# Weight loads cut into 64-row blocks over 128 partitions, with the bulk loads in one queue in order of need and a head built tile by tile

## The chip, the cores and the metric

The kernel runs on one core of a Trainium2 chip. The metric is the device time of one execution in microseconds (us). Each time is a median, with the lowest and highest run beside it. Profiles are of one execution. The profile calls the engines PE (TensorE, matmul), PEld (weight loads into TensorE), DVE (VectorE), ACT (ScalarE), POOL (GpSimd) and SP (SyncE). A trailing q (SPq, ACTq) names the engine's sequencer, where DMA issues appear. The kernel before ran in 207.21 us (two runs, 206.26 and 208.16).

## The reference

Layer norm of x (2048 x 448), then two branches, joined at the end. Types are bf16.

```python
def _A_ref(x, ...):                 # a diagonal state-space layer, P = 448 complex states
    dt = jnp.exp(log_dt); Lam_bar = jnp.exp(dt * Lam)
    Bu = jnp.einsum("bld,pd->blp", x, B_bar)
    for t in range(L): h = Lam_bar * h + Bu[:, t, :]
    return 2.0 * jnp.einsum("blp,dp->bld", hseq, Cmat).real + x * Dskip

def _B_ref(x, w_gate, w_up, w_down):   # a gated feed-forward, F = 1792
    h = _sigmoid(x @ w_gate) * (x @ w_up)
    return h @ w_down

xn = _layernorm(x)
out = x + _A_ref(xn, ...) * _silu(_B_ref(xn, w_gate, w_up, w_down))
```

`w_gate` and `w_up` are 448 x 1792 in DRAM, 1.6 MB each. They must be on chip before TensorE can work on the second branch.

## The kernel before

The kernel records its operations with `add(engine, cost, fn, reads, writes)`. A small scheduler (`Plan`) then orders them on each engine, by costs. So an edit of one line can also move operations that the edit doesn't name.

The contraction over 448 runs in seven steps of 64 rows. Partitions 0 to 63 hold the weights of columns 0 to 895, partitions 64 to 127 those of columns 896 to 1791. That lets two 64-row matmuls run beside each other (lines 603 and 604 of the kernel before). One "step" `m` is 7 + 7 such matmuls; it needs columns `m` of all seven row blocks.

```python
BLK = [(0, 3), (3, 7)]

def load_w(eng, k, half, b):          # one load = one 64-partition half, seven row blocks
    m0, m1 = BLK[b]
    ps = slice(half * H, half * H + H)                    # H = 64
    c0 = half * 896
    load(eng, [("w", k, half, m) for m in range(m0, m1)], ...,
         wgt[k][ps, :, m0 * P:m1 * P],
         wsrc[k][:, c0 + m0 * P:c0 + m1 * P].rearrange("(s p) f -> p s f", p=H))

load_x(0, 1); load_x(1, 1); load_x(2, 2)          # on SP
load_w("ACT", "g", 1, 0); load_w("SP", "g", 0, 0) # gate
load_w("ACT", "g", 1, 1); load_w("SP", "g", 0, 1)
load_w("ACT", "u", 1, 0); load_w("SP", "u", 0, 0) # up
load_w("SP", "u", 1, 1);  load_w("SP", "u", 0, 1)
# ... (cut)
pe_transpose(0); g_head(0, 1)                     # gate steps 0 to 2 on tile 0
pe_transpose(1); g_head(1, 2)                     # the same on tile 1
pe_transpose(2); pe_transpose(3)
columns()
for m in range(3):
    gu_mm(0, "g", m, slots0[m], 2, 4, m == 0)     # then on tiles 2 and 3 together
    gu_evac(0, "g", m, slots0[m])
tables(); coeffs()
load_x(4, 4)                                      # behind all the weights, on SP
b_load()
load("POOL", "wd", F * D * 2, wd[:], ...)         # w_down, on GpSimd's queue
load_x(8, 8, "POOL")
```

Of the kernel before, what the change touches and what calls it, by code (L numbers as in the profile page):

```python
# [18 lines left out]
D = 448  # L19
F = 1792  # L20
P = 128
# [51 lines left out]
class Plan:  # L73
# [53 lines left out]
    def solve(self, pe_from):  # L127
# [11 lines left out]
        for o in reversed(self.ops):  # L139
            for b, kind in o.suc:  # L140
                x = b.late - self._gap(o, b, kind) - o.cost
                if kind is not None and o.eng != b.eng:
                    x -= 1.5 if o.dma else 0.2
                o.late = min(o.late, x)
# [8 lines left out]
        while todo:  # L153
# [13 lines left out]
            if o.dma:  # L167
                q = dma_free[e] = max(dma_free.get(e, 0.0), o.end + 1.2) + o.dma / 200e3
                o.lat = q + 0.6 - o.end
# [13 lines left out]
def kernel(  # L183
# [73 lines left out]
    one = sb.tile([1, 1], BF16, name="one")  # L257
    pio2 = sbt("pio2", [1], FP32)
    vrow = hF_raw[0][0:1, 0:2048].rearrange("p (a b) -> p a b", a=4)
# [27 lines left out]
    def load(eng, key, nbytes, o, i, cost=0.45):  # L287
        e = {"SP": Q, "ACT": A, "POOL": G}[eng]
        add(eng, cost, lambda: e.dma_start(out=o, in_=i), w=[key] if not isinstance(key, list) else key,
            dma=nbytes, chain=True)  # L290

    def load_x(t0, n, q="SP"):
        load(q, [("x", t) for t in range(t0, t0 + n)], n * P * D * 2,
             x_all[:, t0:t0 + n, :], x_src[:, t0:t0 + n, :])

    BLK = [(0, 3), (3, 7)]

    def load_w(eng, k, half, b):
        m0, m1 = BLK[b]
        ps = slice(half * H, half * H + H)  # L300
        c0 = half * 896
        load(eng, [("w", k, half, m) for m in range(m0, m1)], H * 7 * (m1 - m0) * P * 2,
             wgt[k][ps, :, m0 * P:m1 * P],
             wsrc[k][:, c0 + m0 * P:c0 + m1 * P].rearrange("(s p) f -> p s f", p=H))
# [5 lines left out]
    add("POOL", 0.3, lambda: G.memset(warm[:], 0.0), w=["warm"])  # L310
# [3 lines left out]
    add("POOL", 0.1, lambda: G.memset(one[:], 1.0), w=["one"])  # L314
# [6 lines left out]

    add("ACT", 1.3, lambda: A.preload_act_table_set("sqrt_and_others"), w=["sqrttab"], chain=True)
    load_x(0, 1)
    load_x(1, 1)
    load_x(2, 2)
    load_w("ACT", "g", 1, 0)
    load_w("SP", "g", 0, 0)
    load_w("ACT", "g", 1, 1)
    load_w("SP", "g", 0, 1)
    load_w("ACT", "u", 1, 0)  # L330
    load_w("SP", "u", 0, 0)
    load_w("SP", "u", 1, 1)
    load_w("SP", "u", 0, 1)
    for k, vec in enumerate((A_log_dt, A_Lambda_im, A_Lambda_re, A_Dskip)):
        load("POOL", ("vrow", k), D * 2, vrow[:, k, 0:448], vec.unsqueeze(0), cost=1.0)


    def warm_mm(n):
# [3 lines left out]
        add("PE", 0.35 * n, f, r=["warm"], w=[("gu", 2)])  # L342
# [7 lines left out]
    def chain(t0, n):  # L350
# [4 lines left out]
        if t0 < TPC:  # L355
            add("DVE", 0.09, lambda: V.tensor_single_scalar(out=ve, in_=var, scalar=EPS, op=ALU.add), r=ks("mv"), w=ks("ve"))
            add("ACT", 0.2, lambda: A.activation(sd, ve, ACT.Sqrt), r=ks("ve") + ["sqrttab"], w=ks("sd"))
            add("DVE", 0.09, lambda: V.tensor_copy(out=meanf[:, t0:t0 + n, :], in_=mean), r=ks("mv"), w=ks("mf"))
# [9 lines left out]
    def norm(t):  # L368
        b = t % NXN
        if t < TPC:  # L370
# [4 lines left out]
            add("DVE", 0.085, lambda: V.tensor_copy(out=xn[b][:, 448:512], in_=xn[b][:, 0:64]),  # L375
# [18 lines left out]
    def pe_transpose(t):  # L394
# [3 lines left out]
        def f():  # L398
            for s in range(7):
                T.transpose(tp[:, s, :], xn[b][:, s * H:s * H + P], ident[:, :])  # L400
        add("PE", 0.43, f, r=[("xn", b), ("xnw", b), "ident"], w=[("acc", a)])
        add("ACT", 0.476, lambda: A.copy(out=xnT[0][:, 0:4, js], in_=tp[:, 0:4, :]),
            r=[("acc", a)], w=[("xnT", 0, t, "a")])
        add("DVE", 0.27, lambda: V.tensor_copy(out=xnT[0][:, 4:7, js], in_=tp[:, 4:7, :]),
            r=[("acc", a)], w=[("xnT", 0, t, "b")])
# [23 lines left out]
    def columns():  # L429
        a = next_acc()  # L430
        vps = flat(acc[a][:, 0:16], 4, 4)
        add("POOL", 0.3, lambda: G.tensor_copy(out=vrow[:, :, 448:512], in_=vrow[:, :, 384:448]),
            r=[("vrow", k) for k in range(4)], w=["vroww"])

        def f():
            for k in range(4):
                for i in range(4):
                    T.matmul(vps[:, k, i:i + 1], lhsT=vrow[:, k, i * P:(i + 1) * P], rhs=one[:], start=True, stop=True)
# [552 lines left out]
```

## Time and profile before

| what | kernel before |
|---|---|
| time, median (lowest to highest) | 207.21 us (206.26 to 208.16) |
| span of the profiled run, mean clock | 204.8 us, 0.979 |
| TensorE busy, VectorE busy | 186.2 us, 160.0 us |
| first gate matmul | 11.68 us |
| first gate step on all 512 columns | 22.03 us |
| first up step | 28.07 us |

The first view is the table of windows of the kernel before. Each row is a stretch in us from the start, then the stretch's length, the busy time of each engine with its count of instructions, the clock granted to TensorE as a share of full speed, the mean busy share of the core's 16 DMA engines, and GB/s moved.

```profile
core 0: us, PE busy (x) PEld busy (x) DVE busy (x) ACT busy (x) POOL busy (x), PEclk, DMA share, GB/s
0.00:5.00 5.00, 3.69 (x9) 1.34 (x10) 1.02 (x4) 1.49 (x2) 4.38 (x17) 1.00 0.57 141
5.00:10.00 5.00, 1.43 (x11) 0.59 (x9) 2.84 (x11) 0.72 (x2) 0.78 (x1) 0.84 1.12 236
10.00:15.00 5.00, 3.28 (x49) 2.92 (x50) 3.10 (x15) 0.41 (x2) 1.76 (x3) 0.50 1.08 292
15.00:20.00 5.00, 3.34 (x80) 2.96 (x81) 1.15 (x4) 2.19 (x4) 0.20 (x1) 0.98 1.03 333
20.00:25.00 5.00, 5.00 (x66) 3.44 (x64) 3.04 (x8) 4.97 (x7) 3.43 (x7) 1.00 1.10 238
25.00:30.00 5.00, 5.00 (x49) 2.58 (x46) 1.18 (x3) 3.05 (x4) 2.52 (x6) 1.00 1.40 191
```

Look at the last two columns. From 5 to 30 us all the DMA engines are taken (a share of about 1, which can go above 1 where records overlap) and 191 to 333 GB/s flow. The head is bound by data. TensorE is full only from 20 us.

The second view is the list of waits of TensorE in the kernel before (engine, line, what it waited for, us in total, times, longest).

```profile
PE gu L603 <- DMA wG<-in_B_w_gate_dram: 4.1, 1, 4.1
PE gu L603 <- ACT hF L619: 2.4, 1, 2.4
```

TensorE waits 4.1 us for the gate weights, once, and 2.4 us for a tanh on ScalarE.

The third view is part 6 of the page of the kernel before: transfers by target and source, issuing queue, count, KB each and median us from issue to landing.

```profile
wd<-in_B_w_down_dram POOLq DMA_DIRECT2D x1, 1568.0 KB, 13.6
wU<-in_B_w_up_dram SPq DMA_DIRECT2D x2, 448.0 KB, 19.4
...
x_all<-in_A_x_dram SPq DMA_DIRECT2D x1, 448.0 KB, 19.2
```

The second group of x tiles (4 to 7) stands behind the up weights on SP and lands 19.2 us after its issue. The fourth view, VectorE's timeline in the kernel before (start, duration, instruction, in brackets the idle time ahead of it and what ended it), shows VectorE in that wait:

```profile
28.82 1.15 DVE L347 BATCH_NORM_STATS2 bst<-x_all 128x6 f32<-128x448 bf16 x2 [4.07 <-DMA x_all<-in_A_x_dram]
```

### The profile page before, as it was taken

Reading aid. Unit: us, or ns where it says so; the run is one execution under the profiler, and the core shown is the slowest. Engines: PE = TensorE matmul, PEld = TensorE weight load, DVE = VectorE, ACT = ScalarE, POOL = GpSimd, SP = SyncE. Lnnn points to the kernel's source line nnn. Section 1 sums busy time; section 2 is a strip of 40 time slices with the busy share of each in tenths; the row PEclk is TensorE's granted clock in tenths of the full one; section 3 lists DMA queues with packets and bytes.
Section 4 is the critical chain, followed back from the end, with each engine's and each line's share of the span. In section 5 each row is a group of like instructions: output and inputs, shape, how many; then the busy total and the mean of one; then the engine's idle time right before and its main releaser. Section 6 shows DMA issues by size and latency. Waiting matters only on the chain.

```text
span 204.8 us, 3700 instructions
## 1 busy us (share of the span) xinstructions
PE 186.2 (91%) x1459; PEld 92.5 (45%) x1459; DVE 160.0 (78%) x304; ACT 114.6 (56%) x160; POOL 43.4 (21%) x94
## 2 busy tenths in 40 slices
PE   7267995899799999999699999999999999999992
PEld 2156652434344544444244544444445444455561
DVE  1552539999999999999999999995599799531153
ACT  2114947948999956734935943836537582510330
POOL 8130749677100017007106100000000000000000
PEclk9859999999999999999999999999999999999998
DMA  5999994345400013300311220000000000001002
GB/s 143 235 295 338 223 165 88 74 91 109 89 2 3 0 22 71 78 12 3 73 40 45 48 67 0 3 22 22 0 16 10 0 3 22 22 27 48 0 22 67
DMA packets 26946, 13.32 MB, mean 65 GB/s; under 512 B 19696, under 2 KB 26368, under 8 KB 26928
## 3 DMA queue, kind: packets, MB, share of 16 engines
q1 hardware_dynamic: 24800, 9.41, 21.6%
q0 software_dynamic: 736, 2.53, 3.9%
q10 hardware_dynamic: 1392, 1.15, 2.6%
q8 instruction: 11, 0.18, 0.4%
q14 instruction: 7, 0.06, 0.1%
HBM read 6.66 MB, written 1.84 MB: 41 GB/s over the span
## 4 chain that ended last, share of the span: by engine, by line
PE 50%; DVE 23%; DMA 13%; ACT 5%; POOL 4%; issue 2%; SPq 1%; DVEq 0%; POOLq 0%; ACTq 0%
PE gu L603 18%; DMA x_all<-in_A_x_dram 13%; PE acc L782 10%; PE acc L810 8%; PE gu L782 5%; PE gu L667 4%; DVE wv L721 4%; DVE hF L628 3%; DVE bst L347 2%; ACT sig L622 2%; DVE hF L633 2%; DVE cT L572 2%; POOL rsd L364 1%; PE acc L816 1%; POOL sdb L363 1%
## 5 line engine op out<-in xcount | busy, mean ns | idle before, releaser
L603 PE MATMUL gu<-xnT,wG 64*128 64x512 bf16 (+2 forms) x238 | 47.7, 347 | 5.0 <-DMA wG<-in_B_w_gate_dram 4.1
L603 PE MATMUL gu<-xnT,wU 64*128 64x512 bf16 x196 | 46.5, 376 | 2.4 <-ACT hF L619 2.4
L604 PE MATMUL gu<-xnT,wG 64*128 64x512 bf16 (+2 forms) x238 | 47.7, 347 | 0.0
L604 PE MATMUL gu<-xnT,wU 64*128 64x512 bf16 x196 | 46.5, 376 | 0.0
L782 PE MATMUL acc<-wd,hF 128*128 128x448 bf16 x168 | 33.8, 353 | 0.0
L603 PEld LDWEIGHTS <-wG 64*128 64x128 bf16 x238 | 21.4, 98 | 25.4 <-DMA wG<-in_B_w_gate_dram 4.2
L782 PEld LDWEIGHTS <-hF 128*128 128x128 bf16 x224 | 21.5, 98 | 21.3 <-issue 2.1
L622 ACT ACTIVATE sig<-gu 128x1024 bf16<-128x1024 f32 x21 | 21.5, 1022 | 14.5 <-PE gu L604 12.1
L603 PEld LDWEIGHTS <-wU 64*128 64x128 bf16 x196 | 17.9, 94 | 22.8 <-issue 2.1
L632 ACT CAST ub<-gu 128x1024 bf16<-128x1024 f32 x21 | 21.2, 1009 | 9.2 <-PE gu L604 9.1
L810 PE MATMUL acc<-cT,hT 128*128 128x448 bf16 x105 | 24.3, 353 | 0.0
L721 DVE TENSOR_TENSOR_SCAN wv<-c_r,st,z 128x512 bf16<-128x512 f32 x18 | 23.0, 1280 | 0.2
L604 PEld LDWEIGHTS <-wG 64*128 64x128 bf16 x238 | 21.1, 98 | 1.2 <-issue 1.0
L604 PEld LDWEIGHTS <-wU 64*128 64x128 bf16 x196 | 17.7, 94 | 3.3 <-issue 3.2
L633 DVE TENSOR_TENSOR hF<-sig,ub 128x1024 bf16<-128x1024 bf16 x21 | 14.2, 681 | 5.8 <-ACT ub L632 5.8
L347 DVE BATCH_NORM_STATS2 bst<-x_all 128x6 f32<-128x448 bf16 x16 | 9.4, 616 | 10.0 <-DMA x_all<-in_A_x_dram 10.0
L667 PE MATMUL gu<-xnT,bT 128*128 128x512 bf16 x72 | 16.9, 380 | 0.0
L792 DVE TENSOR_TENSOR g_t<-zb,sigd 128x448 bf16<-128x448 bf16 x16 | 6.1, 386 | 12.8 <-ACT zb L791 12.8
L678 ACT CAST bus<-gu 128x1024 bf16<-128x1024 f32 x12 | 12.1, 1010 | 4.8 <-PE gu L667 4.8
L810 PEld LDWEIGHTS <-hT 128*128 128x128 bf16 x119 | 10.4, 98 | 7.3 <-issue 0.4
L790 ACT ACTIVATE sigd<-acc 128x448 bf16<-128x448 f32 x12 | 6.5, 540 | 12.2 <-PE acc L782 12.2
L378 ACT ACTIVATE xn<-x_all,nmr,rsd 128x448 bf16<-128x448 bf16 x12 | 8.8, 754 | 5.6 <-POOL nmr L366 5.6
(140 smaller groups left out, 278.9 us busy)
## 6 DMA issues: line engine op xcount, KB each, us to landing
out_dram<-o_t SPq DMA_DIRECT2D x15, 112.0 KB, 1.7
wd<-in_B_w_down_dram POOLq DMA_DIRECT2D x1, 1568.0 KB, 13.6
wU<-in_B_w_up_dram SPq DMA_DIRECT2D x2, 448.0 KB, 19.4
x_all<-in_A_x_dram POOLq DMA_DIRECT2D x1, 896.0 KB, 11.4
wG<-in_B_w_gate_dram ACTq DMA_DIRECT2D x1, 448.0 KB, 6.9
wG<-in_B_w_gate_dram SPq DMA_DIRECT2D x1, 448.0 KB, 14.9
x_all<-in_A_x_dram SPq DMA_DIRECT2D x1, 448.0 KB, 19.2
xnT<-xn SPq DMA_TRANSPOSE x24, 2.4
```

The costliest lines, as they stand in the source:

```text
L347: add("DVE", 0.53, lambda: V.bn_stats(out=bst[b][:], in_=x_all[:, t, :]), r=[("x", t)], w=[("bst", b)])
L378: add("ACT", 0.65, lambda: A.activation(xn[b][:, 0:448], x_all[:, t, :], ACT.Identity, bias=nmr[:, t, :], scale=rsd[:, t, :]), r=[("x", t) ...
L603: T.matmul(gu[a][:, 0, ts], lhsT=w_[0:H, s, ms], rhs=x[0:H, s, ts], start=(s == 0), stop=(s == 6))
L604: T.matmul(gu[a][:, 1, ts], lhsT=w_[H:P, (s + 1) % 7, ms], rhs=x[H:P, s, ts], start=(s == 0), stop=(s == 6))
L622: add("ACT", act(1024), lambda: A.activation(sig[b][:], gu[a][:], ACT.Sigmoid), r=[("gu", a), "sinL", "cosL", "sth", "cth"] + [(s, p) for ...
L632: add("ACT", act(1024), lambda: A.copy(out=ub[b][:], in_=gu[a][:]), r=[("gu", a)], w=[("ub", b)])
L633: add("DVE", dve2(1024), lambda: V.tensor_tensor(out=ho, in0=sig[sb_][:], in1=ub[b][:], op=ALU.mult), r=[("sig", sb_), ("ub", b)], w=hk)
L667: T.matmul(gu[a][:, i, :], lhsT=bT[:, kt, i, pt * P:pt * P + P], rhs=x[:, 2 * kt, :], start=False, stop=(kt == 2))
L678: add("ACT", act(1024), lambda u=u, a=a: A.copy(out=bus[u][:], in_=gu[a][:]), r=[("gu", a)], w=[("bus", u)])
L721: dve(1.194, lambda k=k: V.tensor_tensor_scan(out=wv[:, k, :], data0=rb, data1=z[:, k, :], initial=(st[pt][:, k, :] if c else 0.0), op0=AL ...
L782: T.matmul(d, lhsT=hF[c % 2][:, m, h, js], rhs=wd[:, ft, :], start=(ft == 0), stop=(ft == FT - 1))
L810: T.matmul(y, lhsT=hT[c % 2][:, hm, js], rhs=cT[:, cm, c0:c1], start=(i == 0), stop=(i == 6))
```

## The change

The intent has four parts. (1) Load the weights by 64-row blocks. One load now brings both column halves of a block, to all 128 partitions, so there are 21 loads of 96 to 224 KB where there were eight of 336 to 448 KB. (2) Put the bulk loads in one queue, SP, in order of need: x tiles 0 to 3 and the first gate blocks (these alternate between SP and ACT), the other gate blocks, x tiles 4 to 7, the up blocks, then `w_down` and the rest of x. (3) Start gate work tile by tile, as each of the first four tiles arrives. (4) Move small work between VectorE, GpSimd and ScalarE.

```diff
-    def load_w(eng, k, half, b):
-        m0, m1 = BLK[b]
-        ps = slice(half * H, half * H + H)
-        c0 = half * 896
-        load(eng, [("w", k, half, m) for m in range(m0, m1)], H * 7 * (m1 - m0) * P * 2,
-             wgt[k][ps, :, m0 * P:m1 * P],
-             wsrc[k][:, c0 + m0 * P:c0 + m1 * P].rearrange("(s p) f -> p s f", p=H))
+    def load_w(eng, k, s, m0, m1):
+        n = (m1 - m0) * P
+        src = wsrc[k][s * H:s * H + H, :].rearrange("p (h c) -> p h c", h=2)[:, :, m0 * P:m1 * P]
+        load(eng, [("w", k, s, m) for m in range(m0, m1)], P * n * 2,
+             wgt[k][:, s, m0 * P:m1 * P], src.rearrange("p h c -> h p c"))
 ... (cut)
+    for t in range(4):
+        load_x(t, 1, ("SP", "ACT")[t % 2])
+    for s in range(7):
+        load_w(("SP", "ACT")[s % 2], "g", s, 0, 3)
     add("ACT", 1.3, lambda: A.preload_act_table_set("sqrt_and_others"), ...)
-    load_x(0, 1)  ...  load_w("SP", "u", 0, 1)          # all of the old order
 ... (cut)
+    for s in range(7):
+        load_w("SP", "g", s, 3, 7)
+    load_x(4, 4)
+    for s in range(7):
+        load_w("SP", "u", s, 0, 7)
 ... (cut)
     pe_transpose(0)
+    pe_transpose(1)
     g_head(0, 1)
-    pe_transpose(1)
+    pe_transpose(2)
     g_head(1, 2)
-    pe_transpose(2)
     pe_transpose(3)
+    g_head(2, 3)
+    for m in range(3):
+        gu_mm(0, "g", m, slots0[m], 3, 4, False)
+        gu_evac(0, "g", m, slots0[m])
     columns()
+    gu_step(0, 3)
 ... (cut: small column arithmetic from POOL to VectorE, copies from VectorE to POOL,
      whole evacuations of tiles 1 to 3 to ScalarE, new cost figures for the scheduler)
-    load("POOL", "wd", F * D * 2, wd[:], ...)
-    load_x(8, 8, "POOL")
+    stats_for(1); prepare(1)
+    load("SP", "wd", F * D * 2, wd[:], ...)
+    c_load()
+    load_x(8, 4); load_x(12, 4)
```

In the kernel before, the source pattern of a weight load, read from the built program (step and count of each dimension, outermost first), is `[[1792,64],[114688,7],[1,n]]`: 64 rows outermost. With the change it is `[[896,2],[1792,64],[1,n]]`: 2 column halves outermost. "Outermost count" below is the count of that first, slowest dimension: 64.

More of the change, by code (lines that the diff above doesn't have):

```diff
@@ L142, in solve @@
                 if kind is not None and o.eng != b.eng:
-                    x -= 1.5 if o.dma else 0.2
+                    x -= 1.5 if o.dma else 1.2 if o.eng == "POOL" else 0.2
                 o.late = min(o.late, x)
@@ L167, in solve @@
             if o.dma:
-                q = dma_free[e] = max(dma_free.get(e, 0.0), o.end + 1.2) + o.dma / 200e3
-                o.lat = q + 0.6 - o.end
+                q = dma_free[0] = max(dma_free.get(0, 0.0), o.end + 1.2) + o.dma / 280e3
+                o.lat = q + (0.6 if e != "POOL" else 5.0) - o.end
             todo -= 1
@@ L256 @@
     ident = sbt("ident", [P])
-    one = sb.tile([1, 1], BF16, name="one")
     pio2 = sbt("pio2", [1], FP32)
-    vrow = hF_raw[0][0:1, 0:2048].rearrange("p (a b) -> p a b", a=4)
+    vrow = hF_raw[0][0:4, 0:512]
     mv = sbt("mv", [NT, 2])
@@ L284, with load, load_x @@
     tag = lambda *k: k
-    def load(eng, key, nbytes, o, i, cost=0.45):
+    def load(eng, key, nbytes, o, i, cost=0.45, r=()):
         e = {"SP": Q, "ACT": A, "POOL": G}[eng]
         add(eng, cost, lambda: e.dma_start(out=o, in_=i), w=[key] if not isinstance(key, list) else key,
-            dma=nbytes, chain=True)
-    def load_x(t0, n, q="SP"):
+            r=r, dma=nbytes, chain=True)
+    def load_x(t0, n, q="SP", r=()):
         load(q, [("x", t) for t in range(t0, t0 + n)], n * P * D * 2,
-             x_all[:, t0:t0 + n, :], x_src[:, t0:t0 + n, :])
-    BLK = [(0, 3), (3, 7)]
-    def load_w(eng, k, half, b):
-        m0, m1 = BLK[b]
-        ps = slice(half * H, half * H + H)
-        c0 = half * 896
-        load(eng, [("w", k, half, m) for m in range(m0, m1)], H * 7 * (m1 - m0) * P * 2,
-             wgt[k][ps, :, m0 * P:m1 * P],
-             wsrc[k][:, c0 + m0 * P:c0 + m1 * P].rearrange("(s p) f -> p s f", p=H))
+             x_all[:, t0:t0 + n, :], x_src[:, t0:t0 + n, :], r=r)
+    def load_w(eng, k, s, m0, m1):
[3 more added lines that the diff above has]
+             wgt[k][:, s, m0 * P:m1 * P], src.rearrange("p h c -> h p c"))
     def tload(keys, o, i, nbytes, r=(), chain=True):
         add("SP", 1.2, lambda: Q.dma_start_transpose(out=o, in_=i), r=r, w=keys, dma=nbytes * 1.5, chain=chain)
-    add("POOL", 0.3, lambda: G.memset(warm[:], 0.0), w=["warm"])
+    add("DVE", 0.2, lambda: V.memset(warm[:], 0.0), w=["warm"])
     add("POOL", 0.15, lambda: G.memset(ident[:], 0.0), w=["ident"])
@@ L313 @@
                                              pattern=[[-1, P]], channel_multiplier=1), r=["ident"], w=["ident"])
-    add("POOL", 0.1, lambda: G.memset(one[:], 1.0), w=["one"])
     add("POOL", 0.1, lambda: G.memset(halfc[:], 0.5), w=["consts"])
@@ L320 @@
                                     allow_small_or_imprecise_dtypes=True), w=[("wv", 0)])
+    for t in range(4):
+        load_x(t, 1, ("SP", "ACT")[t % 2])
+    for s in range(7):
+        load_w(("SP", "ACT")[s % 2], "g", s, 0, 3)
     add("ACT", 1.3, lambda: A.preload_act_table_set("sqrt_and_others"), w=["sqrttab"], chain=True)
-    load_x(0, 1)
-    load_x(1, 1)
-    load_x(2, 2)
-    load_w("ACT", "g", 1, 0)
-    load_w("SP", "g", 0, 0)
-    load_w("ACT", "g", 1, 1)
-    load_w("SP", "g", 0, 1)
-    load_w("ACT", "u", 1, 0)
-    load_w("SP", "u", 0, 0)
-    load_w("SP", "u", 1, 1)
-    load_w("SP", "u", 0, 1)
-    for k, vec in enumerate((A_log_dt, A_Lambda_im, A_Lambda_re, A_Dskip)):
-        load("POOL", ("vrow", k), D * 2, vrow[:, k, 0:448], vec.unsqueeze(0), cost=1.0)
+    for k, vec in enumerate((A_log_dt, A_Lambda_im, A_Lambda_re, A_Dskip)):
+        load("POOL", ("vrow", k), D * 2, vrow[k:k + 1, 0:448], vec.unsqueeze(0), cost=0.8)
+    for s in range(7):
[3 more added lines that the diff above has]
+        load_w("SP", "u", s, 0, 7)
     def warm_mm(n):
@@ L341, in f @@
                 T.matmul(gu[2][:, 0, :], lhsT=warm[:, 0:P], rhs=warm[:], start=True, stop=True)
-        add("PE", 0.35 * n, f, r=["warm"], w=[("gu", 2)])
+        add("PE", 0.43 * n, f, r=["warm"], w=[("gu", 2)])
     def stats(t):
@@ L357, in chain @@
             add("ACT", 0.2, lambda: A.activation(sd, ve, ACT.Sqrt), r=ks("ve") + ["sqrttab"], w=ks("sd"))
-            add("DVE", 0.09, lambda: V.tensor_copy(out=meanf[:, t0:t0 + n, :], in_=mean), r=ks("mv"), w=ks("mf"))
+            add("POOL", 0.15, lambda: G.tensor_copy(out=meanf[:, t0:t0 + n, :], in_=mean), r=ks("mv"), w=ks("mf"))
             add("DVE", 0.09, lambda: V.reciprocal(out=rs, in_=sd), r=ks("sd"), w=ks("rs"))
@@ L374, in norm @@
                 r=[("x", t), ("mf", t), ("rs", t)], w=[("xn", b)])
-            add("DVE", 0.085, lambda: V.tensor_copy(out=xn[b][:, 448:512], in_=xn[b][:, 0:64]),
+            add("POOL", 0.19, lambda: G.tensor_copy(out=xn[b][:, 448:512], in_=xn[b][:, 0:64]),
                 r=[("xn", b)], w=[("xnw", b)])
@@ L396, in pe_transpose, with f @@
         tp = flat(acc[a][:].bitcast(BF16)[:, 0:7 * P], 7, P)
-        def f():
-            for s in range(7):
+        def f(s0, s1):
+            for s in range(s0, s1):
                 T.transpose(tp[:, s, :], xn[b][:, s * H:s * H + P], ident[:, :])
-        add("PE", 0.43, f, r=[("xn", b), ("xnw", b), "ident"], w=[("acc", a)])
-        add("ACT", 0.476, lambda: A.copy(out=xnT[0][:, 0:4, js], in_=tp[:, 0:4, :]),
-            r=[("acc", a)], w=[("xnT", 0, t, "a")])
-        add("DVE", 0.27, lambda: V.tensor_copy(out=xnT[0][:, 4:7, js], in_=tp[:, 4:7, :]),
-            r=[("acc", a)], w=[("xnT", 0, t, "b")])
+        add("PE", 0.36, lambda: f(0, 6), r=[("xn", b), "ident"], w=[("acc", a)])
+        add("PE", 0.06, lambda: f(6, 7), r=[("xnw", b), ("xn", b), "ident", ("acc", a)], w=[("acc", a)])
+        if t == 0:
+            add("ACT", 0.476, lambda: A.copy(out=xnT[0][:, 0:4, js], in_=tp[:, 0:4, :]),
+                r=[("acc", a)], w=[("xnT", 0, t, "a")])
+            add("DVE", 0.27, lambda: V.tensor_copy(out=xnT[0][:, 4:7, js], in_=tp[:, 4:7, :]),
+                r=[("acc", a)], w=[("xnT", 0, t, "b")])
+        else:
+            add("ACT", 0.8, lambda: A.copy(out=xnT[0][:, :, js], in_=tp[:, :, :]),
+                r=[("acc", a)], w=[("xnT", 0, t, "a"), ("xnT", 0, t, "b")])
     def dma_transpose(t):
@@ L431, in columns @@
         vps = flat(acc[a][:, 0:16], 4, 4)
-        add("POOL", 0.3, lambda: G.tensor_copy(out=vrow[:, :, 448:512], in_=vrow[:, :, 384:448]),
-            r=[("vrow", k) for k in range(4)], w=["vroww"])
+        add("POOL", 0.3, lambda: G.tensor_copy(out=vrow[:, 448:512], in_=vrow[:, 384:448]),
+            r=[("vrow", k) for k in range(4)] + [("xnw", 3)], w=["vroww"])
         def f():
-            for k in range(4):
-                for i in range(4):
-                    T.matmul(vps[:, k, i:i + 1], lhsT=vrow[:, k, i * P:(i + 1) * P], rhs=one[:], start=True, stop=True)
-        add("PE", 1.0, f, r=["vroww", "one"] + [("vrow", k) for k in range(4)], w=[("acc", a)])
+            for i in range(4):
+                T.matmul(vps[:, i, :], lhsT=vrow[:, i * P:(i + 1) * P], rhs=ident[0:4, 0:4], start=True, stop=True)
+        add("PE", 0.5, f, r=["vroww", "ident"] + [("vrow", k) for k in range(4)], w=[("acc", a)])
         pv = sbt("pv", [4, 4], FP32)
-        add("DVE", 0.1, lambda: V.tensor_copy(out=pv[:], in_=vps[:]), r=[("acc", a)], w=["pv"])
+        add("DVE", 0.1, lambda: V.tensor_copy(out=pv[:].rearrange("p k i -> p i k"), in_=vps[:]), r=[("acc", a)], w=["pv"])
         dt_b = C("dt", 4, BF16)
@@ L448, in pool, with small @@
             add("POOL", cost, fn, r=r, w=w)
-        tt = lambda o, x, y, op: (lambda: G.tensor_tensor(out=o, in0=x, in1=y, op=op))
+        def small(fn, r, w):
+            add("DVE", 0.1, fn, r=r, w=w)
+        tt = lambda o, x, y, op: (lambda: V.tensor_tensor(out=o, in0=x, in1=y, op=op))
         theta, arg, turn, r_col = C("theta"), C("arg"), C("turn"), C("r")
-        pool(tt(theta[:], dt_b[:], lim, ALU.mult), ["dt", "pv"], ["theta"])
-        pool(lambda: G.tensor_single_scalar(out=turn[:], in_=theta[:], scalar=1.0 / TWO_PI, op=ALU.mult),
+        small(tt(theta[:], dt_b[:], lim, ALU.mult), ["dt", "pv"], ["theta"])
+        small(lambda: V.tensor_single_scalar(out=turn[:], in_=theta[:], scalar=1.0 / TWO_PI, op=ALU.mult),
              ["theta"], ["turn"])
-        pool(lambda: G.tensor_single_scalar(out=turn[H:P, 3:4], in_=theta[H:P, 3:4], scalar=-1.0 / TWO_PI,
+        small(lambda: V.tensor_single_scalar(out=turn[H:P, 3:4], in_=theta[H:P, 3:4], scalar=-1.0 / TWO_PI,
                                             op=ALU.mult), ["theta", "turn"], ["turn"])
-        pool(tt(arg[:], dt_b[:], lre, ALU.mult), ["dt", "pv"], ["arg"])
+        small(tt(arg[:], dt_b[:], lre, ALU.mult), ["dt", "pv"], ["arg"])
         add("ACT", 0.2, lambda: A.activation(r_col[:], arg[:], ACT.Exp), r=["arg"], w=["r"])
@@ L607, in gu_mm @@
         return add("PE", 7 * (0.0028 + n / 2400.0) + (2 * SW if first else 0), f,
-                   r=xr(c, lo, hi) + [("w", k, 0, m), ("w", k, 1, m)], w=[("gu", a)], name=f"{k}{c}.{m}")
+                   r=xr(c, lo, hi) + [("w", k, s, m) for s in range(7)], w=[("gu", a)], name=f"{k}{c}.{m}")
     sg_n = [0]
@@ L836, in whole @@
         ssm_pair(c, 2)
-    warm_mm(12)
+    warm_mm(9)
     for t in range(4):
@@ L850, with stats_for @@
     pe_transpose(0)
+    pe_transpose(1)
     g_head(0, 1)
-    pe_transpose(1)
+    pe_transpose(2)
     g_head(1, 2)
-    pe_transpose(2)
     pe_transpose(3)
+    g_head(2, 3)
+    for m in range(3):
+        gu_mm(0, "g", m, slots0[m], 3, 4, False)
+        gu_evac(0, "g", m, slots0[m])
     columns()
-    for m in range(3):
-        gu_mm(0, "g", m, slots0[m], 2, 4, m == 0)
-        gu_evac(0, "g", m, slots0[m])
+    gu_step(0, 3)
     tables()
     coeffs()
-    load_x(4, 4)
     b_load()
-    load("POOL", "wd", F * D * 2, wd[:], B_w_down.rearrange("(ft p) d -> p ft d", p=P), cost=1.0)
-    load_x(8, 8, "POOL")
-    for t in range(4, 16):
-        stats(t)
-        if t % 2 == 1:
-            chain(t - 1, 2)
-        if t == 7:
-            prepare(1)
-            c_load()
-    for i in range(3, 13):
+    def stats_for(c):
+        for t in range(4 * c, 4 * c + 4):
+            stats(t)
+            if t % 2:
+                chain(t - 1, 2)
+    stats_for(1)
+    prepare(1)
+    load("SP", "wd", F * D * 2, wd[:], B_w_down.rearrange("(ft p) d -> p ft d", p=P))
+    c_load()
+    load_x(8, 4)
+    load_x(12, 4)
+    for i in range(4, 13):
         gu_step(0, i)
+    stats_for(2)
+    stats_for(3)
     b_units(0, (0, 1))
```

## The prediction

> What bounds it now. The page gives PE 186.2 of 204.8 us, VectorE 160.0. By stretches (table of windows) three regimes follow: up to 22 us PE waits for data; from 33 to 97 us VectorE is full (21.37 of 22, 24.70 of 25, 19.68 of 20 us) and PE nearly so; after 100 us PE is full (25.00 of 25 three times). So nothing idles later than 33 us that could absorb a late start: a shift of both PE and VectorE in the head passes almost whole to the end.
>
> The head, from the timeline and the waits of PE. The first gate matmul starts at 11.68 us, after a 4.07 us wait for wG; by then all of wG (1.6 MB), four x tiles and part of wU have shared the queues. The granted clock was 0.50 in 10 to 15 us, so the first 42 matmuls took 2.25 us against 1.45 at full clock. The fourth gate step (full 512 columns) starts at 22.03, the first up step at 28.07. x tiles 4 to 7 land 19.2 us after issue, at 28.8 us, behind wU on the same queue; VectorE, in order, stands 4.07 us there, the sine tables and then ACT's tanh come late, and PE waits 2.4 us for that tanh.
>
> What the change does. (1) Order of need: x 0-3 and the first wG block (1.15 MB) first. At the 141 GB/s of the first 5 us and 236 of the next that lands at about 7.5 us, not 11.7: 3.5 to 4 us. Wake-up gap shorter, so the clock probably stays up: 0.8 us. (2) Tile-wise head: four groups of 1.45 us instead of two and a 2.4 us group: +0.5 us of PE, but no wait for the last pair; three evacuations go whole to ACT (about 0.85 us), copies of 0.14 and 0.18 us leave VectorE. I expect the fourth gate step at 15 to 16 us (-6 to -7). (3) x 4-7 before wU: VectorE's 4.07 us and PE's 2.4 us wait go. (4) Small column arithmetic on VectorE: adds under 1 us, removes POOL hops. (5) Wd and the rest of x come after that on SP, needed only after 45 us.
> PE-limited gain 8 to 9 us at the second up step; VectorE reaches its table work (31.4 us now) about as much earlier. Taking off 1 to 2 us for new bumps: about 7 us, 200.5 us.
>
> The danger. Each weight load now reads a DRAM pattern whose outermost count is 2 (half, row, column). The Trainium skill, "DMA: Bandwidth & Descriptors", section "Rules for kernel authors", recommends one 128-partition transfer over two halves, but also says a slowest dimension smaller than 16 confines a DMA to at most that many engines. No load in this trace has such a pattern, so the trace cannot decide. If it holds here, two engines at the 15 to 20 GB/s each seen now carry 3.2 MB: wG would end at about 40 us, wU at 80, the first up step would slip by 50 us and the time would be 240 to 270 us. I give this about 0.2, since the schedule looks tuned around 280 GB/s.
>
> What would show it: first gate matmul at 7 to 8 us; PE clock near 1 through 20 us; x 4-7 landing before 15 us; no wait of PE for tanh; VectorE full from about 24 us. Wrong if weight loads land tens of us late with low GB/s (danger true), if ACT's five DMA issues delay the first square root past 7 us, or if VectorE's full stretch keeps its old end at 97 us. The stretch after 100 us should look the same.
>
> Prediction 200.5 us, 80% range 196 to 206; faster by over 2% 0.66, within 2% 0.12, slower 0.22.

## The result and the profile after

| what | before | after |
|---|---|---|
| time, median (lowest to highest) | 207.21 us (206.26 to 208.16) | 251.72 us (250.56 to 252.87) |
| span of the profiled run, mean clock | 204.8 us, 0.979 | 248.8 us, 0.880 |
| first gate matmul | 11.68 us | 9.97 us |
| first gate step on 512 columns | 22.03 us | 28.87 us |
| first up step | 28.07 us | 45.95 us, its last weight block at 71.76 us |

The kernel after is slower: the ratio is 1.2148, with a 95% interval from 1.181 to 1.2485. Ratios in this document are the mean time of one kernel's fast runs over that of the other's of the same rounds, so they are not quite the ratio of the quoted medians.

The table of windows of the kernel after, same columns as above:

```profile
5.00:10.00 5.00, 1.20 (x17) 0.84 (x17) 3.45 (x16) 3.12 (x7) 2.13 (x9) 0.82 0.13 44
10.00:15.00 5.00, 0.76 (x7) 0.23 (x7) 0.38 (x1) 0.00 (x0) 0.40 (x2) 0.50 0.14 47
15.00:20.00 5.00, 0.64 (x10) 0.38 (x12) 0.00 (x0) 0.00 (x0) 0.00 (x0) 0.50 0.14 47
20.00:25.00 5.00, 5.00 (x83) 4.41 (x78) 0.00 (x0) 0.91 (x1) 0.00 (x0) 0.50 0.15 51
25.00:30.00 5.00, 3.98 (x100) 3.17 (x98) 0.00 (x0) 4.39 (x5) 0.00 (x0) 0.98 0.14 48
...
45.00:60.00 15.00, 2.90 (x14) 0.59 (x9) 4.09 (x9) 7.92 (x12) 7.77 (x14) 0.64 0.13 51
```

The DMA share fell from about 1.1 to 0.13 to 0.15. Two sixteenths are 0.125. The rate fell from 236 to 333 GB/s to 44 to 51. The engines were not full: most of them were not used. The waits of TensorE in the kernel after:

```profile
PE gu L603 <- DMA wU<-in_B_w_up_dram: 22.4, 6, 3.9
PE gu L603 <- DMA wG<-in_B_w_gate_dram: 16.3, 7, 3.9
```

TensorE's timeline in the kernel after, at the first up step, one matmul pair per weight block:

```profile
45.95 0.37 PE L602 MATMUL gu<-xnT,wU 64*128 64x512 bf16 x1 [0.24 <-ACT hF L618]
49.13 0.60 PE L603 MATMUL gu<-xnT,wU 64*128 64x512 bf16 x1 [2.81 <-DMA wU<-in_B_w_up_dram]
...
53.66 0.61 PE L603 MATMUL gu<-xnT,wU 64*128 64x512 bf16 x1 [3.92 <-DMA wU<-in_B_w_up_dram]
...
58.18 0.61 PE L603 MATMUL gu<-xnT,wU 64*128 64x512 bf16 x1 [3.91 <-DMA wU<-in_B_w_up_dram]
...
71.76 0.60 PE L603 MATMUL gu<-xnT,wU 64*128 64x512 bf16 x1 [3.92 <-DMA wU<-in_B_w_up_dram]
```

In the kernel before, the same step runs without a wait (its first and its seventh pair):

```profile
28.07 0.38 PE L603 MATMUL gu<-xnT,wU 64*128 64x512 bf16 x1
...
29.36 0.38 PE L603 MATMUL gu<-xnT,wU 64*128 64x512 bf16 x1
```

A block of the up weights (128 x 896 x 2 B = 229,376 B) comes every 4.52 us: 50.7 GB/s. If two engines carry it, that is 25.4 GB/s each. The matmul behind each such wait takes 0.60 us instead of 0.37. This is the clock: the Trainium skill, "TensorE: Matmul & The Clock Gate", section "HAM oscillation — how this bites in real kernels", says that waits of more than about 3.4 us between short bursts throttle TensorE again and again, and this trace agrees (waits of 3.9 us, granted clock 0.64 in 45 to 60 us). The wait of 2.81 us, below that figure, was followed by a 0.60 us matmul too.

SyncE's timeline in the kernel after shows the same from the issuing side:

```profile
1.63 29.11 SPq L288 DMA_DIRECT2D wG<-in_B_w_gate_dram  x11
30.78 2.60 SPq L288 DMA_DIRECT2D x_all<-in_A_x_dram  x1
33.42 25.85 SPq L288 DMA_DIRECT2D wU<-in_B_w_up_dram  x7
```

The queue accepts only as fast as the engines drain it: x tiles 4 to 7 are not issued before 30.78 us and land at 40.0, and VectorE stands 29.7 us at its statistics for them.

Nearly all of the loss is in the head. The last matmul pair of the first up step starts at 29.36 us before and at 71.76 us after, 42.4 us later. From there to the end it is 204.8 − 29.4 = 175.4 us before and 248.8 − 71.8 = 177.0 us after.

### The profile page after: what moved, and what is told of

Read it like the earlier page. It is cut to its first block, busy times and chain, and to the rows that moved or that the text cites. A ratio compares the mean times of both kernels' runs of the same rounds, so it can differ in the third digit from the quotient of the medians.

```text
span 248.8 us, 3769 instructions
## 1 busy us (share of the span) xinstructions
PE 195.4 (79%) x1486; PEld 93.3 (38%) x1486; DVE 158.8 (64%) x298; ACT 115.9 (47%) x160; POOL 43.0 (17%) x94
## 4 chain that ended last, share of the span: by engine, by line
PE 43%; SPq 25%; DVE 12%; DMA 10%; ACT 4%; POOL 3%; issue 2%; POOLq 0%; ACTq 0%; DVEq 0%
SPq L288 21%; PE gu L602 15%; PE acc L781 9%; DMA wU<-in_B_w_up_dram 7%; PE acc L809 6%; PE gu L781 4%; SPq L302 4%; PE gu L666 3%; DMA x_all<-in_A_x_dram 3%; PE gu L603 3%; DVE wv L720 2%; DVE hF L627 1%; DVE bst L339 1%; ACT xn L370 1%; POOL rsd L356 1%
## 5 line engine op out<-in xcount | busy, mean ns | idle before, releaser
L603 PE MATMUL gu<-xnT,wU 64*128 64x512 bf16 x196 | 50.3, 396 | 22.4 <-DMA wU<-in_B_w_up_dram 22.4
L603 PE MATMUL gu<-xnT,wG 64*128 64x512 bf16 (+1 forms) x259 | 52.0, 349 | 16.3 <-DMA wG<-in_B_w_gate_dram 16.3
L602 PE MATMUL gu<-xnT,wG 64*128 64x512 bf16 (+1 forms) x259 | 52.1, 349 | 2.4 <-DMA wG<-in_B_w_gate_dram 1.7
L602 PE MATMUL gu<-xnT,wU 64*128 64x512 bf16 x196 | 50.4, 396 | 0.2 <-ACT hF L618 0.2
L603 PEld LDWEIGHTS <-wG 64*128 64x128 bf16 x259 | 22.7, 103 | 22.7 <-DMA wG<-in_B_w_gate_dram 18.8
L603 PEld LDWEIGHTS <-wU 64*128 64x128 bf16 x196 | 18.5, 97 | 31.9 <-DMA wU<-in_B_w_up_dram 25.9
L602 PEld LDWEIGHTS <-wG 64*128 64x128 bf16 x259 | 22.7, 103 | 20.6 <-issue 2.4
L602 PEld LDWEIGHTS <-wU 64*128 64x128 bf16 x196 | 18.4, 97 | 18.9 <-issue 2.1
L627 DVE SCALAR_TENSOR_TENSOR hF<-hF,gu 128x1024 bf16<-128x1024 bf16 x7 | 8.5, 1220 | 24.1 <-issue 23.9
L666 PE MATMUL gu<-xnT,bT 128*128 128x512 bf16 x72 | 18.1, 400 | 0.0
L354 POOL TENSOR_SCALAR veb<-mv 128x2 bf16<-128x2 bf16 x6 | 2.6, 427 | 69.4 <-DVE mv L340 69.3
L485 ACT ACTIVATE cosT<-hT,pio 128x512 bf16<-128x512 f32 x3 | 2.2, 722 | 25.2 <-DVE hT L479 25.2
```

Of the source, the lines that this page charges most:

```text
L602: T.matmul(gu[a][:, 0, ts], lhsT=w_[0:H, s, ms], rhs=x[0:H, s, ts], start=(s == 0), stop=(s == 6))
L603: T.matmul(gu[a][:, 1, ts], lhsT=w_[H:P, (s + 1) % 7, ms], rhs=x[H:P, s, ts], start=(s == 0), stop=(s == 6))
L666: T.matmul(gu[a][:, i, :], lhsT=bT[:, kt, i, pt * P:pt * P + P], rhs=x[:, 2 * kt, :], start=False, stop=(kt == 2))
```

## The experiments

Theory: the outermost count of the source, 2, confines each load to two DMA engines. Rivals: (a) the small row pieces (768 to 1,792 B) going to 128 partitions are slow by themselves; (b) many small loads in one queue are slow; (c) the new order or the tile-wise head is at fault. A second question is what the change is worth without its fault.

### The outermost count: 4, 8 and 16

The three kernels change only the source pattern. The built programs stand in the same order as the kernel after on every engine, and number, size, target and queue of all loads are the same. The pattern reads overlapping rows, so the result is wrong; the timing is what was asked.

```diff
-        src = wsrc[k][s * H:s * H + H, :].rearrange("p (h c) -> p h c", h=2)[:, :, m0 * P:m1 * P]
+        w = wsrc[k]
+        r0 = min(s * H, 296)
+        src = bass.AP(tensor=w.tensor, offset=w.offset + r0 * F + m0 * P,
+                      ap=[[40 * F, 4], [F, 32], [1, n]])
```

For 8 the pattern is 8 x 16 rows, for 16 it is 16 x 8 rows (`[[10 * F, 16], [F, 8], [1, n]]`).

> Wrong result on purpose: the changed kernel with each weight load reading 4 groups of 32 rows instead of 2 groups of 64; same number of loads, bytes, run lengths, queues and order, only the outermost count of the DRAM pattern goes from 2 to 4. Theory (outermost count sets the number of DMA engines): rate while weights load doubles from 51 to about 100 GB/s, DMA share 0.13 to about 0.25, last wU load lands near 40 us instead of 71.7, time about 218 us. Rival 1 (single queue) and rival 2 (many small loads, cost per issue): nothing they name has changed, so about 252 us and 51 GB/s.

> As outer4 with 8 groups of 16 rows. Theory: about 200 GB/s while weights load, share 0.5, last wU load near 23 us, time about 204 us. Rivals: about 252 us.

> As outer4 with 16 groups of 8 rows, wrong result on purpose. Theory: all engines carry the weights, 250 to 330 GB/s, share near 1, last wU load near 18 us, time about 200 us, which is what the prediction's sum gave without the danger. Rivals 1 and 2: about 252 us. If it lands between (say 215) the small loads or the one queue carry a part.

TensorE's timeline with outermost count 4:

```profile
33.75 0.39 PE L606 MATMUL gu<-xnT,wU 64*128 64x512 bf16 x1 [1.88 <-DMA wU<-in_B_w_up_dram]
36.01 0.54 PE L606 MATMUL gu<-xnT,wU 64*128 64x512 bf16 x1 [1.87 <-DMA wU<-in_B_w_up_dram]
38.27 0.60 PE L606 MATMUL gu<-xnT,wU 64*128 64x512 bf16 x1 [1.71 <-DMA wU<-in_B_w_up_dram]
```

The blocks now come every 2.26 us, half of 4.52. The tables of windows of the runs with 4, with 8 and with 16, a row of each:

```profile
25.00:30.00 5.00, 3.52 (x34) 1.76 (x32) 4.63 (x17) 1.98 (x4) 3.10 (x7) 1.00 0.26 101
```

```profile
10.00:15.00 5.00, 5.00 (x83) 4.31 (x81) 0.00 (x0) 0.91 (x1) 0.15 (x1) 0.55 0.73 225
```

```profile
10.00:15.00 5.00, 5.00 (x150) 4.47 (x144) 0.67 (x2) 3.40 (x4) 0.19 (x2) 1.00 0.96 276
```

| outermost count | DMA share | GB/s | packets in flight at once, mean (stretch) | time (one run each, state unknown) |
|---|---|---|---|---|
| 2 (the kernel after) | 0.13 to 0.15 | 44 to 51 | 2.1 (46 to 58 us) | 251.72 us (median of 2) |
| 4 | 0.26 | 101 | 4.2 (25 to 29 us) | 220.72 us |
| 8 | 0.53 to 0.73 | 178 to 225 | 8.7 (8 to 10 us) | 202.32 us |
| 16 | 0.96 | 276 | 15.1 (11 to 13.5 us) | 197.67 us |

The packets are counted from the packet records (start and duration) that each run's trace keeps; the views don't print them. In the kernel after there are exactly two packets in flight for 90% of that stretch, and three in the rest.

Where weight loads alone are under way, share and rate go with the count: n/16 of the engines, 101 GB/s being twice 51. With 8, other loads share some windows, which is why its share exceeds 0.5. Rivals (a), (b) and (c) fall as causes of the large loss: pieces, number of loads, queues, order and head are the same in all four. A packet of 1,792 B took the same 74 ns (median) with counts 2, 4 and 16, so the single pieces are not slower. This is what the Trainium skill, "DMA: Bandwidth & Descriptors", says in the sections "Why a DMA increments its semaphore by 16 and not by 1" (the engines used are the largest number up to 16 that divides the slowest dimension of both patterns) and "Rules for kernel authors" (an outermost size below 16 confines the transfer). Our runs agree at 2, 4, 8 and 16. No record names a single engine, so the number of engines is inferred; share, rate and packets in flight agree on it.

The single 197.67 us with count 16 was later timed as `outer16_timed`, see below. Four later runs took 201.55 to 204.24 us, so it was a lucky run.

### The load form alone, in the kernel before

The opposite test: the kernel before, with only the weight loads in the new form. The result is correct.

```diff
-    load_w("ACT", "g", 1, 0) ... load_w("SP", "u", 0, 1)
+    for k in "gu":
+        for b in BLK:
+            for s in range(7):
+                load_w("SP" if s < 4 else "ACT", k, s, *b)   # load_w as in the kernel after
```

> Correct result: the kernel before, with nothing changed but its weight loads, which take the changed form (7 blocks with outermost count 2 per region, on the two queues). Theory: the loss belongs to the form of the load alone: 51 GB/s while weights load, share near 0.13, wU complete near 65 us, time 240 to 260 us although nothing is on one queue. Rival 1 (one queue for all bulk loads): about 207 us, as two queues are used.

It took 262.49 us (one run, state unknown), a little over the expected range. Its window from 15 to 55 us, and ScalarE's timeline:

```profile
15.00:55.00 40.00, 4.21 (x56) 3.68 (x57) 4.17 (x19) 1.20 (x4) 0.00 (x0) 0.54 0.14 48
```

```profile
0.75 22.12 ACTq L289 DMA_DIRECT2D wG<-in_B_w_gate_dram  x6
22.92 0.20 ACT L353 ACTIVATE sdb<-veb 128x1 bf16<-128x1 bf16 x1 [20.91 <-issue]
```

The form alone makes the loss. Two readings more. Loads on two queues together moved 48 GB/s, not twice 50: the loads of both queues share the same two engines. The packet records of this run agree: from 20 to 50 us there are two packets in flight for 82% of the time and three for nearly all the rest, half of them from each queue. (The skill's page says, in the first of the two sections above, that such a transfer takes the lowest-numbered engines; rate and packets agree, but no record shows engine numbers.) And ScalarE could not compute while its issues were held: its first square root came at 22.92 us. So part of this 262 us is the blocked issuing engine, which the kernel after mostly avoids by using SP.

### The correct repair: halves again, new order kept

The kernel after, but each weight load again one 64-partition half with 64 rows outermost: gate block 1 on SP and ACT, all others on SP in the new order.

```diff
-    for s in range(7):
-        load_w(("SP", "ACT")[s % 2], "g", s, 0, 3)
+    for h in range(2):
+        load_w(("SP", "ACT")[h], "g", h, 0, 3)      # load_w with halves, as before
 ... (the same for the other gate columns and for the up weights, on SP)
```

> Correct result: the changed kernel, but each weight load again takes one 64-partition half with 64 rows outermost (2 loads for the first gate block, 2 for the second, 2 for up), order of need kept. Theory: about 200.5 us (196 to 206), first gate matmul at 7 to 8 us, tiles 4 to 7 of x before 15 us, no wait of PE for weights after the head. If the single queue for bulk loads were the cause, it would stay well above 215 us, since gate block two, x and up are all on SP still.

It took 206.02 us (205.62 to 207.26), ratio 0.9954 [0.9866, 1.0043]: the 45 us are back, the gain is not (196 to 206 was expected). The waits of TensorE in this run say why:

```profile
PE acc L435 <- POOL hF L430: 6.2, 1, 6.2
```

TensorE waits 6.2 us for a small copy of the parameter vectors on GpSimd. GpSimd works in order, and the scheduler had put that copy behind the statistics of x tiles 4 to 7, whose data land at 14.65 us; the copy ran at 20.72. So the next kernel makes those statistics depend on the copy, which puts them behind it:

```diff
-        add("POOL", 0.4, lambda: ... op=ALU.add), r=ks("mv"), w=ks("ve"))
+        add("POOL", 0.4, lambda: ... op=ALU.add), r=ks("mv") + (["vroww"] if t0 < 8 else []), w=ks("ve"))
```

> Correct result: fix_halves with GpSimd's widening copy of the four vectors (the one PE waited 6.2 us for) put ahead of the statistics of x tiles 4 to 7, by one added dependency. Theory: the missing part of the gain in fix_halves is that in-order wait on GpSimd and not the loads, so the 6.2 us wait of PE goes and the time falls by 5 to 6 us to about 200.5 us. Rival: the 64-partition loads themselves cost it (they move 214 to 234 GB/s against 253 to 276 in outer16): then PE waits for weights instead and it stays at 204 to 206 us.

It took 203.39 us (203.19 to 203.51), ratio 0.9831 [0.9786, 0.9875]: 2.6 us less and not the expected 5 to 6, so it missed both the theory and the rival (204 to 206). The wait for GpSimd is gone, and another one has grown (2.4 us in the run before) in the list of VectorE:

```profile
DVE bT L548 <- DMA bT<-in_A_B_im_dram: 4.1, 1, 4.1
```

VectorE, also in order, stands 4.1 us at a copy whose data come late, ahead of the sine tables. The next kernel puts that copy behind the tables, again by a dependency:

```diff
-            r=[("bT3", 0), ("bT3", 1)], w=["bT3l"])
+            r=[("bT3", 0), ("bT3", 1)] + [("nu", p) for p in range(4)], w=["bT3l"])
```

> Correct result: fix_halves_pool with VectorE's copy of bT put after the third step of the sine tables (one added dependency), because there VectorE stood 4.09 us for bT and PE then 2.9 us for VectorE. Theory: the halved loads lose only through in-order waits that the schedule did not foresee; VectorE's wait shrinks to about 1 us and the time falls by 2 to 3 us to about 200.5 to 201.5 us. Rival: the loads are the limit, the wait moves to another instruction, within 1 us of 203.4.

It took **199.18 us (198.4 to 200.85), ratio 0.9632 [0.9564, 0.97]**, correct, and it beats both kernels. VectorE's wait for that copy shrank to 2.1 us (about 1 was expected), and TensorE's wait of 2.9 us for VectorE is gone. The fall of 4.2 us is more than the 2 to 3 expected, and not all of it is shown to be the copy's: the scheduler moved other operations too, and in the two profiles the first up step is already 0.8 us apart (25.35 and 24.58 us). Its table of windows:

```profile
5.00:10.00 5.00, 3.14 (x55) 2.74 (x56) 3.74 (x16) 1.90 (x5) 2.32 (x10) 0.82 1.11 261
10.00:15.00 5.00, 5.00 (x132) 4.40 (x128) 0.81 (x2) 2.64 (x3) 0.23 (x1) 0.84 1.10 230
15.00:20.00 5.00, 2.51 (x41) 1.41 (x36) 3.37 (x14) 3.39 (x5) 3.77 (x8) 1.00 1.17 213
```

The rate is 213 to 261 GB/s, no more than before. The gain is in what comes first: TensorE's first gate matmul is at 8.06 us (11.68 before), the first gate step on 512 columns at 16.54 (22.03), x tiles 4 to 7 are used from 14.2 (28.82).

### Two queues instead of one, and smaller loads

The best version, with the second halves of the later gate columns and of the up weights on ACT's queue instead of SP's:

```diff
-        load_w("SP", "g", h, 3, 7)
+        load_w(("SP", "ACT")[h], "g", h, 3, 7)
-        load_w("SP", "u", h, 0, 7)
+        load_w(("SP", "ACT")[h], "u", h, 0, 7)
```

> Correct result: fix_halves_dve with the second halves of the second gate block and of up issued by ACT, so that both halves move at once on two queues. Theory: one 64-partition half at a time moves slower (214 to 234 GB/s in fix_halves at 10 to 20 us) than two at once (324 GB/s in the kernel before at 12 to 22 us); at 10 to 20 us this run shows 280 GB/s or more, x tiles 4 to 7 land later because the up half of ACT is beside them, time 199 to 202 us. Rival: half at a time is not slower, the lower rate came from the transposes among them, and nothing improves (within 1 us of fix_halves_dve, either way).

It took 200.89 us (200.43 to 201.91), ratio 0.9694 [0.9632, 0.9756]. The expected rate of 280 GB/s was missed (258 and 189 in 10 to 20 us). A second queue gives no more rate over these 10 us here, and the interval overlaps that of one queue. The packet records show that the limit with halves isn't a lack of engines. In fix_halves_dve from 10 to 14 us 17.6 packets are in flight on average, but a packet of 1,024 B takes 87 ns. It took 46 ns with outermost count 16 (8 to 10 us, 10.9 in flight), and 54 ns in the kernel before while `w_down` moved beside it (12 to 16 us, 16.5 in flight). Why it takes longer with one half under way was not tested.

The kernel after, with each block load cut in two 64-partition loads of 48 to 112 KB, which keeps the block order and has 64 rows outermost:

```diff
+        for h in range(2):
+            c0 = h * 896
+            load(eng, [("w", k, s, m, h) for m in range(m0, m1)], H * n * 2,
+                 wgt[k][h * H:h * H + H, s, m0 * P:m1 * P],
+                 wsrc[k][s * H:s * H + H, c0 + m0 * P:c0 + m1 * P])
```

> Correct result: the changed kernel with each 128-partition weight load cut into two 64-partition loads of 64 rows by n columns, so 42 weight loads instead of 21, each 48 to 112 KB. Theory (engine count): all 16 engines carry them, about 250 GB/s, time 198 to 203 us. Rival 2 (small loads, cost per issue): twice as many loads would be slower than the changed kernel's 252 us, or at least stay above 230 us.

It took 206.75 us (206.25 to 207.26), ratio 0.9994 [0.9945, 1.0043]: over the expected range, but with more and smaller loads 45 us below the kernel after, which rules out (b) once more and with a correct result. SyncE's timeline in this run:

```profile
1.64 15.70 SPq L288 DMA_DIRECT2D wG<-in_B_w_gate_dram  x22
```

Twenty-two issues take 15.70 us, 0.71 us each with the gaps; in the steady part one takes 0.59 us and the next starts 0.64 us after it. From 6 to 16 us the DMA share is only 0.40, at 103 GB/s: 64 KB per issue cannot fill the engines from one queue. The Trainium skill, "DMA: Bandwidth & Descriptors", section "Issuing engines are not separate DMA queues", calls the time to start a DMA usually small beside the DMA. In this run it is not: it is the limit.

### The order of need alone, in the kernel before

First only x tiles 4 to 7 ahead of the up weights:

```diff
     load_w("SP", "g", 0, 1)
+    load_x(4, 4)
     load_w("ACT", "u", 1, 0)
 ... (cut)
-    load_x(4, 4)
```

> Correct result: the kernel before with nothing changed but x tiles 4 to 7 loaded ahead of wU. Theory of the prediction's step 3: VectorE's 4.07 us wait and PE's 2.4 us wait go, the time falls by 2 to 4 us to 203 to 205 us. Rival: later waits take it back, within 1 us of 207.

It took 211.08 us (210.41 to 212.67), ratio 1.0228 [1.0154, 1.0301]: no gain but a loss of 1.5 to 3%. From part 6 of its page, and from TensorE's waits:

```profile
wd<-in_B_w_down_dram POOLq DMA_DIRECT2D x1, 1568.0 KB, 13.4
...
x_all<-in_A_x_dram SPq DMA_DIRECT2D x1, 448.0 KB, 18.6
```

```profile
PE gu L604 <- DMA wG<-in_B_w_gate_dram: 6.4, 1, 6.4
```

The tiles were used from 22.8 us instead of 28.8, but from issue to landing they still took 18.6 us, while `w_down` on GpSimd's queue, first used at 63.5 us in this run, was under way at the same time (360 GB/s in 15 to 20 us). And the gate weights came later: TensorE's wait rose from 4.1 to 6.4 us. The next kernel tests whether `w_down` held them: it also takes `w_down` and the last x tiles off GpSimd's queue, to SP's, behind the up weights:

```diff
-    load("POOL", "wd", F * D * 2, wd[:], ...)
-    load_x(8, 8, "POOL")
 ... (cut)
+            load("SP", "wd", F * D * 2, wd[:], ...)     # on SP, behind the up weights, ahead of C
+            load_x(8, 8)                                # on SP, behind C
```

> Correct result: the kernel before with x tiles 4 to 7 ahead of up as in before_x4, and also wd and x tiles 8 to 15 taken from GpSimd's queue to the end of SP's, so that they no longer share the engines with the first weights. Theory: before_x4 lost because wd on another queue (issued at 4.6 us) still took the bandwidth; now x tiles 4 to 7 land near 15 us instead of 22.8, the wait of PE for wG falls below 4.07 us, time 202 to 205 us. Rival: the emitted order of VectorE in before_x4 is the cause, and it stays at 209 to 212 us.

It took 205.72 us (204.61 to 206.78), ratio 0.9936 [0.9865, 1.0007]. The tiles now land after 11.4 us, at 15.2 instead of 28.8, and the wait for the gate weights is 3.9 us, so the other queue's bulk was what delayed both in before_x4. Yet the time (202 to 205 expected) is the same within the interval. VectorE now waits 6.5 us, once, for a result of GpSimd (7.0 us in the run before this one), a wait that the kernel before doesn't have. So order of need alone, without the earlier first gate block and the tile-wise head, is worth 1.4% at most by that interval.

### What the whole change is worth with all engines

The kernel with outermost count 16 once more, timed. It is the change itself without its fault (wrong, as above).

> Wrong result on purpose: outer16 again, now in timed rounds against the kernel before, for an interval. Theory: 197 to 199 us, ratio about 0.955. If the one run of before was a stroke of luck of the clock, 200 us or more.

It took 203.51 us (201.55 to 204.24), ratio 0.9815 [0.9741, 0.989], not the 197.67 of the single run. ScalarE's timeline, then TensorE's, then a row of the windows:

```profile
47.05 0.67 ACT L571 ACTIVATE ctmp<-xnT,c_n2i 128x448 f32<-128x448 bf16 x1 [4.25 <-DMA xnT<-in_A_C_im_dram]
```

```profile
56.94 0.58 PE L656 MATMUL gu<-xnT,bT 64*128 64x512 bf16 x1 [3.26 <-ACT ub L634]
```

```profile
55.00:65.00 10.00, 6.76 (x26) 3.18 (x27) 9.38 (x15) 8.94 (x13) 1.15 (x3) 0.66 0.00 0
```

ScalarE stands 4.25 us for the transposed C matrix, which is queued behind `w_down` on SP. Some 10 us later TensorE waits 3.26 us for ScalarE, and its clock is down: 0.66 on average in 55 to 65 us. That the first wait makes the second is argued from the order here. In the lucky run ScalarE's wait was 1.92 us. Two more kernels put the C transposes ahead of `w_down`, in this kernel and in the best correct one:

```diff
-    load("SP", "wd", F * D * 2, wd[:], ...)
     c_load()
+    load("SP", "wd", F * D * 2, wd[:], ...)
```

> The all-engine timing variant (result wrong on purpose, as in outer16_timed), with the two C transposes issued ahead of w_down on the one queue; nothing else changed. Theory (the wait of ScalarE for C_im, 4.25 us in outer16_timed, makes TensorE wait 3.26 us and costs the clock): ScalarE's wait for C_im is under 1 us, the mean clock from 55 to 65 us is above 0.9 instead of 0.66, and the time is 199 to 201 us, 2.5 to 4 us below the 203.5 of outer16_timed. Rival (something else in the new order keeps it at 203): the wait goes but the time stays at 202.5 to 204.

> The best correct version (fix_halves_dve, 199.2 us), with the two C transposes issued ahead of w_down; nothing else changed. There ScalarE had no wait for C, so the theory expects no gain: 198.5 to 200.5 us, same as fix_halves_dve. The rival (C ahead of w_down is worth something by another road) expects 197 us or less.

With count 16 it took 200.55 us (199.39 to 201.56), ratio 0.9687 [0.9599, 0.9775]. ScalarE's wait for C is 1.9 us (expected: under 1), the clock in 55 to 65 us is 1.00, and the time is in the expected range. The lucky run had the same 1.9 us without the edit, so one profile doesn't show that the edit shortened the wait; the times of the four runs each hardly touch (199.39 to 201.56, 201.55 to 204.24). In the best correct version it took 202.67 us (201.52 to 202.75), ratio 0.9763 [0.9699, 0.9828]; 198.5 to 200.5 was expected, so this missed. TensorE's timeline in that last run:

```profile
48.90 0.37 PE L654 MATMUL gu<-xnT,bT 64*128 64x512 bf16 x1 [2.08 <-ACT sig L622]
```

The scheduler answered the edit by moving the C work on ScalarE ahead of a sigmoid. ScalarE waited 1.46 us for C, and TensorE then 2.08 us for the sigmoid. That isn't the whole of the loss: in the two profiles the first up step is already 1.1 us apart (25.64 and 24.58 us), before any operation that the edit moved. So the same edit gained about 1.3% in one kernel and lost about 1.3% in the other (0.9687 against 0.9815, 0.9763 against 0.9632). These pairs were timed in different rounds and their intervals touch or overlap, so the size is rough. "C ahead of `w_down`" is no rule. What cost time in these traces is an in-order engine that waits while TensorE needs it.

## Why the prediction was wrong

The time was predicted at 200.5 us, 196 to 206, and it was 251.72. Step by step:

- **What bounds the kernel before.** Right: the head waits for data, and a shift of the head passes to the end almost whole. From the last pair of the first up step on, the two kernels take 175.4 and 177.0 us.
- **The danger.** This is the step that failed, and it failed by its weight, not its mechanism. The central estimate takes the weight loads at the rates of the kernel before: in step (1), 1.15 MB move at "the 141 GB/s of the first 5 us and 236 of the next" and land "at about 7.5 us". The kernel after moved 99 and then 44 GB/s in these stretches, and TensorE still waited for a part of that first gate block at 19.75 us. The case in which two engines carry the weights was seen and set aside. The prediction says: "I give this about 0.2, since the schedule looks tuned around 280 GB/s." The danger was true. The mechanism held (outermost counts 2, 4, 8, 16 give shares of about n/16). The size held: 240 to 270 us was named, 251.72 came. The first up step began 17.9 us later, at 45.95, and its last pair came at 71.76, 42.4 us behind that of before (29.36); 50 was named. Each engine carried 25.4 GB/s and not the assumed 15 to 20, so the gate ended at about 39 us (40 named) and the first up step got its last block at 72 (80 named). The figure of 280 GB/s that argued against the danger is a number that the change gave the scheduler. It is not a measurement, and it should have weighed nothing against a rule that fitted the access pattern exactly.
- **Step 1, first gate matmul at 7 to 8 us.** It came at 9.97 in the kernel after; with all engines at work it came at 7.82 (count 16) and 8.06 (the repaired version). About right but for the danger.
- **Step 2, fourth gate step at 15 to 16 us.** 28.87 in the kernel after, 15.77 (count 16) and 16.54 (the repaired version) with all engines. About right but for the danger.
- **Step 3, x tiles 4 to 7 ahead of the up weights takes VectorE's 4.07 us and TensorE's 2.4 us away.** Not as a step by itself: in the kernel before it gave 211.08 us alone, and 205.72 with the other queue cleared too. In the kernel after it did the opposite, since those tiles stood behind the slow gate loads: VectorE waited 29.7 us for them.
- **The sum, 7 us of gain.** With the fault taken out it is roughly right. The change with count 16 gave 203.51 us, 200.55 with C moved forward; the repaired correct version gave 206.02, then 203.39, then 199.18 as TensorE's wait of 6.2 us for GpSimd was taken away and VectorE's of 4.1 us cut to 2.1. "Taking off 1 to 2 us for new bumps" was too little for what the scheduler produced at first: the bumps took all or half of the gain.
- **The stretch after the head unchanged.** Right.

Still open: why one run of the count 16 kernel took 197.67 us and four others 201.55 to 204.24. The wait for C differs between the two traces (1.92 and 4.25 us), but what makes C land late or early from run to run was not tested.

## What to carry to other kernels

Before you turn two loads into one, write down the outermost count of both access patterns: here a rearrangement that put two column halves outermost cut the rate from 191 to 333 down to 44 to 51 GB/s, and the halves it replaced, in the new order and with two added dependencies, gave the fastest correct kernel (199.18 us against 207.21 and 251.72). Read the DMA share beside the rate: here a share of 0.13 to 0.15, about two sixteenths, while TensorE waited for weights, came from a pattern that didn't spread, not from a full queue. And when a reordering gives less than its sum, look for an in-order engine that stands at an operation whose data come late while others need what is queued behind it.

## What the Trainium skill lacked or had wrong

- "DMA: Bandwidth & Descriptors", "Rules for kernel authors": the row on two transfers to disjoint partition halves says not to bother and to use one 128-partition transfer. It doesn't say that the merged transfer's source can get an outermost count of 2. Here two halves gave 213 to 261 GB/s and 199.18 us; the merged load gave 44 to 51 GB/s and 251.72 us. The row on using all 16 engines has the rule, but its only example is a broadcast; two column halves of a DRAM matrix are another case.
- The same page, "Specifications", gives about 27 GiB/s per engine (29 GB/s). Worked out from the runs: about 25 GB/s per engine with two or four at work (50.7 over 2, 101 over 4), and 14 to 22 GB/s with all sixteen busy (230 over 16 in fix_halves_dve, 360 over 16 in before_x4).
- The same page, "Issuing engines are not separate DMA queues", calls the issue time usually small. Measured: one issue every 0.64 us, which held a chain of 64 KB loads to 103 GB/s. The section doesn't say that an engine is held at its issue while its earlier loads drain: ScalarE was held 22.12 us by six issues, SyncE 29.11 us by eleven.
- The same page says that spreading loads over queues doesn't add rate; the runs agree (200.89 us with two queues, 199.18 with one). That the queues interleave it says as well, but not what this does to an order of need: a bulk load on another queue delays what is first in this one (x tiles landed 18.6 us after issue with `w_down` beside them, 11.4 us with it behind them).
- "TensorE: Matmul & The Clock Gate", "HAM oscillation — how this bites in real kernels", names gaps of over about 3.4 us. Measured: shorter gaps were already followed by slow matmuls. In the kernel after, waits of 2.34 and 2.40 us (at 33.34 and 36.35 us) were followed by matmuls of 0.60 and 0.61 us (0.37 at full clock), and with outermost count 4 a row of waits of 1.7 to 1.9 us with one matmul pair between them took matmuls from 0.39 to 0.60 us.
